# Padded full-array pair units, a transposed second batch and DMA transposes in a recurrence + mixer kernel

## The chip, the cores and the metric

The kernel runs on one core of one Trainium2 chip. The metric is the device time of one execution in microseconds (us). Before the change the median of three runs is 174.36 us (174.34 to 175.11). A profiled run took 174.75 us; the profile's span, from its first to its last instruction, is 173.0 us, and all positions below are counted from the start of that span.

## The reference

Two parts follow each other. The first is a gated linear recurrence for 4 batches, 8 heads, 768 time steps and a head width of 48. The second is a low-rank mixing over time and an MLP over the 384 channels.

```python
# q, k, v, alpha: (4, 8, 768, 48)
for t in range(S):
    state = alpha[:, :, t, :, None] * state + outer(k[:, :, t], v[:, :, t])   # per batch and head
    y[:, :, t] = q[:, :, t] @ state
x = y as (B, S, 384)
h = (x^T @ U @ V)^T            # U: (768, 32), V: (32, 768)
u = x + h
out = u + max(u @ w_ch1, 0) @ w_ch2      # w_ch1: (384, 1536), w_ch2: (1536, 384)
```

The kernel computes the recurrence in chunks: with the running product of alpha folded into q and k, a chunk's output is q times the state before the chunk, plus a masked (q k^T) times v, and the state is carried on once per chunk.

## The kernel before

Work is not issued in program order. Each operation is added to a plan with the engines that may do it and an estimated cost; the plan then simulates the engines and fixes the order of each engine's instructions before anything is built. A buffer is taken from a pool when the plan reaches its first user. TensorE's modes (whole array, halves, quarters) cost a switch in the plan.

```python
LAT = {"PE": 215.0, "ACT": 155.0, "DVE": 145.0, "POOL": 110.0, "SP": 400.0}
SWITCH = 95.0
TOL = 150.0
...
P.warm_until = 28000.0      # until then gaps on TensorE are filled with products of zeros (line 291)
```

Batches 0 and 1 (`PAIR`) are cut in units of 256 time steps and four heads, two time steps to a partition (j = 0, 1). The two halves of the partitions are two chunks (c = 0, 1) of 128 steps. State update and output are products over 64 partitions, each half into a bank of its own:

```python
P.add({"POOL": 480, "ACT": 420}, lambda e: copy(e, jh(rv()), raw(vt)), ...)         # v to bf16, rows kt, rv
...
db = [Buf(bank) for _ in range(nch)]            # nch = 2 for the first two blocks, 1 for the last
for n in range(4):
    a, j = n // 2, n % 2
    for c in range(nch):
        r = slice(64 * c, 64 * c + 64)
        nc.tensor.matmul(db[c]()[:, a * 2 * D : (a + 1) * 2 * D],                   # line 479
            lhsT=rk()[r, HP * j + 2 * a : HP * j + 2 * a + 2, :]..., rhs=rv()[r, ...]...)
...
yb = Buf(bank), Buf(bank)
# q times the state before the chunk: line 518, 96 columns, whole array
for h in range(HP):
    for j in range(2):
        for c in range(2):
            r = slice(64 * c, 64 * c + 64)
            nc.tensor.matmul(yb[c]()[:, h * D : (h + 1) * D],                       # line 531
                lhsT=pm()[r, (h // 2) * 2 + j, h % 2, :], rhs=rv()[r, HP * j + h, :], ...)
for c in range(2):    # two copies of 192 columns to xb
    P.add({"ACT": 250, "DVE": 265}, ...)
```

Batches 2 and 3 are cut in units of 128 steps and eight heads. In both kinds of unit alpha's logarithm is taken on ScalarE (lines 375 and 547), summed over time on TensorE (384 to 391, 554 to 557), and its exponentials scale k and q to `rk` and `rq` (405, 572). These are transposed on TensorE (418, 584) and copied from PSUM to `kt` and `qt`. Then come the scores (445, 605), their mask on VectorE (456, 615), the state and the output (for batches 2 and 3 lines 628, 662 and 664).

The mixing reads the finished batch (line 681: x times U). Batch 0 builds u transposed directly in PSUM, from products with the identity (700) and the low-rank term (703), and a second time untransposed for the residual. The other batches build u untransposed and transpose it on TensorE:

```python
for c in range(NC):
    hb = Buf(bank, 3 if b == 0 else 0)
    P.add({"PE": mm(DM)}, ... vm_sb x utx ...)                  # line 712
    P.add({"DVE": 465}, ... ub = xb + hb ...)                   # line 713
    if c % 2 == 1 and b > 0:
        ...
        P.add({"PE": mm(*[C] * 6)}, f_tr, ...)                  # line 722: six transposes of 128x128
        P.add({"DVE": 450, "ACT": 710}, f_ev, ...)              # copy to uT
```

The MLP's first stage (line 749) takes 72 products of 384 columns for a batch, with a ReLU out of PSUM on ScalarE or VectorE (759, 761). The second stage (line 772) takes another 72, and VectorE adds the residual (779):

```python
nc.tensor.matmul(hb()[:, 0:TW], lhsT=w1_sb[:, ct, ...], rhs=uT()[:, ct, ...], ...)          # line 749
...
nc.tensor.matmul(hb()[:, 0:DM], lhsT=h1()[:, jt, ...], rhs=w2_sb[:, jt, :], ...)            # line 772
...
P.add({"DVE": 468}, lambda e: nc.vector.tensor_tensor(ou(), ub()[:, c, :], hb()[:, 0:DM], op=ALU.add), ...)
P.add({"SP": 550.0}, lambda e: nc.sync.dma_start(out[b, c * C : (c + 1) * C, :], ou()), ...)
```

All DMAs are issued by SyncE (SP), in the plan's order.

Of the kernel before, what the change touches and what calls it, by code (L numbers as in the profile page):

```python
# [40 lines left out]
class Plan:  # L41
# [4 lines left out]
    TOL = 150.0  # L46
    warm = None
# [41 lines left out]
    def run(self):  # L89
# [10 lines left out]
        while todo:  # L100
# [18 lines left out]
            for eng, ok in per.items():  # L119
                t0 = min(t for t, _ in ok)  # L120
                t1, op = min(((t, o) for t, o in ok if t <= t0 + 1.0), key=lambda x: (x[1].prio, x[1].i))
                key = (t1, t1 + op.engs[eng])
                if best is None or key < best[0]:
                    best = (key, eng, op)
# [12 lines left out]
            if eng == "SP":  # L137
                dma = max(dma, t + 600.0) + cost
                clock[eng] = max(t + 450.0, dma - 3500.0)
                end = dma + 2000.0  # L140
            else:
                if eng == "PE" and op.mode != mode:
                    cost += self.SWITCH
                    mode = op.mode
                clock[eng] = end = t + cost
            order.append(op)
            done = end + self.LAT[eng]
            for b in op.bufs:
                b.left -= 1
                b.last = max(b.last, done)  # L150
                if b.left == 0:
                    b.pool.free[b.idx] = b.last
# [27 lines left out]
def kernel(  # L180
# [33 lines left out]
    PAIR = (0, 1)  # L214
    RES = (1, 1, 1, 0)
# [55 lines left out]
    rvs = Pool(slots("rv", 5, [C, H, D], BF16))  # L271
# [9 lines left out]
    ubs = Pool(slots("ub", 3, [128, NC, DM], BF16))  # L281
# [22 lines left out]
    def small():  # L304
        P.add({"SP": 450.0}, lambda e: nc.sync.dma_start(u_in, moe_U.rearrange("(c p) r -> p c r", p=128)), w=["u_in"], prio=2.5)
        P.add({"SP": 500.0}, lambda e: nc.sync.dma_start(v_in, moe_V), w=["v_in"], prio=2.5)
# [8 lines left out]
    def weight(dst, src, key, prio, pr, engs):  # L315
        t = Buf(io)
        P.add({"SP": 540.0}, lambda e: nc.sync.dma_start(flat(t), src), w=[t], prio=prio)  # L317
        P.add(engs, lambda e: copy(e, dst, flat(t)), r=[t], w=[key], prio=pr)
# [14 lines left out]
    LEAD = 3.0  # L333
    tiles = {}

    def stage_loads(b):
        def load(t, src, c, key):
            if b in PAIR:
                hs, sl = slice((c % 2) * HP, (c % 2 + 1) * HP), slice((c // 2) * 2 * C, (c // 2 + 1) * 2 * C)
                P.add(  # L340
                    {"SP": 750.0},
# [7 lines left out]
            P.add({"SP": 1000.0}, lambda e: nc.sync.dma_start(t(), src[b, :, sl, :].rearrange("h t d -> t h d")), w=[t], prio=key)  # L349
# [11 lines left out]
    def stage_pair(b, u, sprev, xb):  # L361
# [3 lines left out]
        sl = 0.0 if b == 0 else 150.0  # L365
# [10 lines left out]
        rv = Buf(rvs)  # L376
        P.add({"POOL": 480, "ACT": 420}, lambda e: copy(e, jh(rv()), raw(vt)), r=[vt], w=[rv], prio=pr + 20, slack=sl)
# [85 lines left out]
        db = [Buf(bank) for _ in range(nch)]  # L463
# [6 lines left out]
        def f_id(e, c, last):  # L470
            nc.tensor.matmul(db[c]()[:, 0 : 2 * Q // 2], lhsT=ident, rhs=sview(before[c]), start=not last, stop=last, skip_group_check=True)

        def f_d(e):
            for n in range(4):
                a, j = n // 2, n % 2
                for c in range(nch):
                    r = slice(64 * c, 64 * c + 64)
                    more = onpe and c == 1
                    nc.tensor.matmul(
                        db[c]()[:, a * 2 * D : (a + 1) * 2 * D],  # L480
                        lhsT=rk()[r, HP * j + 2 * a : HP * j + 2 * a + 2, :].rearrange("t h w -> t (h w)"),
                        rhs=rv()[r, HP * j + 2 * a : HP * j + 2 * a + 2, :].rearrange("t h d -> t (h d)"),
                        start=(n == 0 and not (onpe and c == 0 and sprev is not None)), stop=(n == 3 and not more), skip_group_check=True,
                    )

        if onpe and sprev is not None:
            P.add({"PE": mm(Q)}, lambda e: f_id(e, 0, False), r=[(sprev, 1)], w=[db[0]], prio=pr + 8, slack=sl)
        P.add({"PE": mm(*[2 * D] * 4)}, f_d, r=[rk, rv], w=db, prio=pr + 8, mode="H", slack=sl)
        for c in range(nch):
# [10 lines left out]
            if onpe or prev is None:  # L500
                if onpe and c == 1:
                    P.add({"PE": mm(Q)}, lambda e: f_id(e, 1, True), r=[(st, 0)], w=[db[1]], prio=pr + 7, slack=sl)
                P.add({"DVE": 270}, lambda e, c=c, f=f_st: f(e, db[c]()[:, 0:Q]), r=[db[c], tot], w=[(st, c)], prio=pr + 4, slack=sl)
            else:
                sm = Buf(sms)
                P.add(
                    {"DVE": 270},
                    lambda e, c=c, sm=sm, prev=prev: nc.vector.tensor_tensor(sm()[:, 0:Q], db[c]()[:, 0:Q], sview(prev), op=ALU.add),
                    r=[db[c], prev], w=[sm], prio=pr + 4, slack=sl,
                )  # L510
                P.add({"POOL": 480, "DVE": 270}, lambda e, sm=sm, f=f_st: f(e, sm()[:, 0:Q]), r=[sm, tot], w=[(st, c)], prio=pr + 4, slack=sl)

        yb = Buf(bank), Buf(bank)

        def f_yi(e, c):
            s = before[c]
            for a in range(2):
                nc.tensor.matmul(
                    yb[c]()[:, 2 * a * D : (2 * a + 2) * D], lhsT=qT()[:, 2 * a + c, :], rhs=s[0]()[:, 2 * s[1] + a, :],
                    start=(a == 0), stop=False, skip_group_check=True,  # L520
                )

        def f_y(e):
            for c in range(2):
                if before[c] is not None:
                    f_yi(e, c)
            for h in range(HP):
                for j in range(2):
                    for c in range(2):
                        r = slice(64 * c, 64 * c + 64)  # L530
                        nc.tensor.matmul(
                            yb[c]()[:, h * D : (h + 1) * D], lhsT=pm()[r, (h // 2) * 2 + j, h % 2, :], rhs=rv()[r, HP * j + h, :],
                            start=(h == 0 and j == 0 and before[c] is None), stop=(h == HP - 1 and j == 1), skip_group_check=True,
                        )

        P.add({"PE": mm(*[2 * D] * 4, *[D] * 8) + 95}, f_y, r=[qT, rv, (pm, 0), (pm, 1)] + [x for x in before if x is not None], w=[yb[0], yb[1]], prio=pr, mode="H", slack=sl)
        for c in range(2):
            P.add({"ACT": 250, "DVE": 265}, lambda e, c=c: copy(e, xb()[:, 2 * blk + c, half * Q : (half + 1) * Q], yb[c]()[:, 0:Q]), r=[yb[c]], w=[(xb, 2 * blk + c, half)], prio=pr, slack=sl)
        return st

    def stage_gla(b, c, sprev, xb):
        kk = b * NC + c
        pr = kk * 100.0
        sl = 150.0
# [33 lines left out]
        tk, tq = Buf(bank), Buf(bank)  # L578
        kT, qT = Buf(kts), Buf(qts)

        def f_tr(ring, tb):
            t = bf(tb()).rearrange("p (e c) -> p e c", c=C)
            for p in range(HP):
                nc.tensor.matmul(  # L584
                    t[:, p, :],
                    lhsT=ring()[:, 2 * p : 2 * p + 2, :].rearrange("t h w -> t (h w)"),
                    rhs=ident, start=True, stop=True, is_transpose=True,
                )

        def f_ev(e, dst, tb):  # L590
            copy(e, dst(), bf(tb()).rearrange("p (e c) -> p e c", c=C)[:, 0:HP, :])

        P.add({"PE": mm(*[C] * 4)}, lambda e: f_tr(rk, tk), r=[rk], w=[tk], prio=pr + 18, slack=sl)
        P.add({"PE": mm(*[C] * 4)}, lambda e: f_tr(rq, tq), r=[rq], w=[tq], prio=pr + 18, slack=sl)
        P.add({"DVE": 335, "ACT": 500}, lambda e: f_ev(e, kT, tk), r=[tk], w=[kT], prio=pr + 8, slack=sl)
        P.add({"DVE": 335, "ACT": 500}, lambda e: f_ev(e, qT, tq), r=[tq], w=[qT], prio=pr + 8, slack=sl)
# [76 lines left out]
    def stage_mix(b, xb, ub, uT):  # L673
        pr = (b * NC + NC - 0.5) * 100.0
        sl = 0.0 if b == 0 else 150.0
# [10 lines left out]
        if b == 0:  # L686
# [6 lines left out]
        if b == 0:  # L693
# [15 lines left out]
            pr = mlp_prio(0, 0.3)  # L709
        for c in range(NC):  # L710
            hb = Buf(bank, 3 if b == 0 else 0)
            P.add({"PE": mm(DM)}, lambda e, c=c, hb=hb: nc.tensor.matmul(hb()[:, 0:DM], lhsT=vm_sb[:, c * C : (c + 1) * C], rhs=utx(), start=True, stop=True), r=[utx, ("vm", c // NT)], w=[hb], prio=pr + c, slack=sl)  # L712
            P.add({"DVE": 465}, lambda e, c=c, hb=hb: nc.vector.tensor_tensor(ub()[:, c, :], xb()[:, c, :], hb()[:, 0:DM], op=ALU.add), r=[hb] + xk(b, xb, c), w=[(ub, c)], prio=pr + c, slack=sl)  # L713
            if c % 2 == 1 and b > 0:
# [18 lines left out]

    def mlp_prio(b, x):
        return ((b + 1) * NC + LEAD + x * NC) * 100.0

    def mlp1(b, uT, h1, tt):
        for jt in range(NJ):
# [3 lines left out]
            if b == 0:  # L742
                need = [(uT, tt, j) for j in range(NCT)]
            else:
# [20 lines left out]
    def mlp2(b, ub, h1, c):  # L765
        hb = Buf(bank, RES[b])
        tt = c // NT
        for g in range(3):

            def f(e, g=g):  # L770
                for jt in range(4 * g, 4 * g + 4):
                    nc.tensor.matmul(  # L772
                        hb()[:, 0:DM], lhsT=h1()[:, jt, c * C : (c + 1) * C], rhs=w2_sb[:, jt, :],
                        start=(jt == 0), stop=(jt == NJ - 1),
                    )

            P.add({"PE": mm(*[DM] * 4)}, f, r=[(h1, tt, jt) for jt in range(4 * g, 4 * g + 4)] + [("w2", jt) for jt in range(4 * g, 4 * g + 4)], w=[hb], prio=mlp_prio(b, 0.5 + c / 12.0 + g / 36.0))
        ou = Buf(outs)
        P.add({"DVE": 468}, lambda e: nc.vector.tensor_tensor(ou(), ub()[:, c, :], hb()[:, 0:DM], op=ALU.add), r=[hb, (ub, c)], w=[ou], prio=-100)  # L779
# [7 lines left out]
    for b in range(B):  # L787
# [7 lines left out]
        stage_mix(b, xb, ub, uT)  # L795
        mlp1(b, uT, h1, 0)
        mlp1(b, uT, h1, 1)
        for c in range(NC):
            mlp2(b, ub, h1, c)
# [33 lines left out]
```

## Time and profile before

| What | Value |
|---|---|
| Median time | 174.36 us |
| Span of the profile | 173.0 us, mean granted TensorE clock 0.986 |
| MLP products (lines 749 and 772) | 288 + 288, 53.1 + 52.8 us in the rows |
| Transposing products (418, 584, 700, 722) | 96 + 96 + 18 + 54 |
| Half-array products (479, 531) | 80 + 192 |
| Additions for u on VectorE (713) | 24, 547 ns each |
| Copies of v on GpSimd | 19, 590 ns each |
| Loads of q, k, v, alpha and the weights | 120 of 192 KB, 4.3 to 4.5 us from issue to landing |
| Output stores | 24 of 192 KB, 1.9 us |

Busy times are given for each engine over the span. PE is TensorE's products, PEld its weight loads, which lie beside the products. DVE is VectorE, ACT ScalarE, POOL GpSimd and SPq the sequencer of SyncE, which only issues DMAs. The profile cuts the span in 40 slices of 4.3 us and gives the busy share of each in tenths. Products on TensorE overlap like a pipeline, so the duration of one in a row is its latency and not the time that it takes from the engine. The chain of waits follows the work that ended last back from its end, at each step to what released it. Windows give busy times by stage.

### The profile page before, as it was taken

Reading aid. Unit: us, or ns where it says so; the run is one execution under the profiler, and the core shown is the slowest. Engines: PE = TensorE matmul, PEld = TensorE weight load, DVE = VectorE, ACT = ScalarE, POOL = GpSimd, SP = SyncE. Lnnn points to the kernel's source line nnn. Section 1 sums busy time; section 2 is a strip of 40 time slices with the busy share of each in tenths; the row PEclk is TensorE's granted clock in tenths of the full one; section 3 lists DMA queues with packets and bytes.
Section 4 is the critical chain, followed back from the end, with each engine's and each line's share of the span. In section 5 each row is a group of like instructions: output and inputs, shape, how many; then the busy total and the mean of one; then the engine's idle time right before and its main releaser. Section 6 shows DMA issues by size and latency. Waiting matters only on the chain.

```text
span 173.0 us, 4823 instructions
## 1 busy us (share of the span) xinstructions
PE 161.9 (94%) x1862; PEld 104.2 (60%) x1862; DVE 109.0 (63%) x232; ACT 104.1 (60%) x247; POOL 59.5 (34%) x97
## 2 busy tenths in 40 slices
PE   7688998899996999999998999999999999999991
PEld 2355765566564776676676657666666566656560
DVE  4589685598996986958675559976474294000231
ACT  4588773779785767558949436638783210996000
POOL 8056366247331765255155414910430000000000
PEclk9999699999999999999999999999999999999998
DMA  5999989999998999999989999611000212100222
GB/s 140 266 249 260 267 255 335 258 300 330 269 267 200 178 207 211 214 222 221 230 147 206 189 166 258 170 58 37 0 0 4 91 45 91 51 0 0 91 93 91
DMA packets 83031, 28.82 MB, mean 167 GB/s; under 512 B 76832, under 2 KB 82976, under 8 KB 83008
## 3 DMA queue, kind: packets, MB, share of 16 engines
q1 hardware_dynamic: 83008, 28.52, 72.0%
q8 instruction: 14, 0.23, 0.6%
q14 instruction: 9, 0.07, 0.2%
HBM read 23.79 MB, written 4.72 MB: 165 GB/s over the span
## 4 chain that ended last, share of the span: by engine, by line
PE 60%; DMA 19%; SPq 15%; issue 2%; POOL 1%; ACT 1%; DVE 0%; ACTq 0%; POOLq 0%
PE ps L772 27%; PE ps L749 16%; SPq L342 10%; DMA io<-in_v_dram 8%; DMA io<-in_moe_w_ch_dram 5%; SPq L317 3%; DMA io<-in_alpha_dram 3%; PE ps L584 3%; DMA io<-in_k_dram 3%; PE ps L605 2%; PE ps L712 2%; PE ps L722 2%; PE ps L664 1%; PE ps L554 1%; PE ps L418 1%
## 5 line engine op out<-in xcount | busy, mean ns | idle before, releaser
L749 PE MATMUL ps<-uT,w_sb 128*128 128x384 bf16 x288 | 53.1, 326 | 0.0
L772 PE MATMUL ps<-w_sb,h1t 128*128 128x384 bf16 x288 | 52.8, 326 | 0.0
L759 ACT ACTIVATE h1t<-ps 128x384 bf16<-128x384 f32 x73 | 35.2, 494 | 8.8 <-PE ps L749 8.5
L772 PEld LDWEIGHTS <-h1t 128*128 128x128 bf16 x288 | 26.1, 98 | 16.0 <-issue 1.0
L749 PEld LDWEIGHTS <-w_sb 128*128 128x128 bf16 x288 | 26.1, 98 | 15.4
L779 DVE TENSOR_TENSOR ou<-ub,ps 128x384 f32<-128x384 bf16 x24 | 13.2, 551 | 27.6 <-PE ps L772 27.3
L302 POOL CAST rv<-io 128x384 bf16<-128x384 f32 x19 | 11.2, 590 | 35.7 <-DMA io<-in_v_dram 30.7
L615 DVE TENSOR_TENSOR pm<-ps,maskc 128x512 bf16<-128x512 f32 x24 | 15.7, 685 | 6.7 <-PE ps L605 6.5
L572 POOL TENSOR_TENSOR rk<-io,ai 128x384 bf16<-128x384 f32 x12 | 11.0, 916 | 20.2 <-ACT ai L565 18.7
L761 DVE TENSOR_SCALAR h1t<-ps 128x384 bf16<-128x384 f32 x23 | 12.6, 552 | 7.4 <-PE ps L749 4.8
L456 DVE TENSOR_TENSOR pm<-ps,maskp 128x512 bf16<-128x512 f32 x24 | 15.8, 681 | 0.7 <-ACT h1t L759 0.5
L298 ACT CAST xb<-ps 128x192 bf16<-128x192 f32 (+1 forms) x23 | 8.8, 392 | 11.6 <-PE ps L664 7.6
L298 ACT COPY kt<-ps 128x512 bf16<-128x512 bf16 x17 | 10.0, 586 | 5.8 <-PE ps L584 5.3
L713 DVE TENSOR_TENSOR ub<-xb,ps 128x384 bf16<-128x384 bf16 x24 | 12.1, 547 | 1.2 <-PE ps L712 1.2
L298 ACT COPY qt<-ps 128x512 bf16<-128x512 bf16 x17 | 11.3, 663 | 1.6 <-PE ps L418 1.0
L302 POOL CAST w_sb<-io 128x384 bf16<-128x384 f32 x21 | 10.8, 527 | 3.8 <-DMA io<-in_moe_w_ch_dram 3.5
L572 POOL TENSOR_TENSOR rq<-io,aa 128x384 bf16<-128x384 f32 x12 | 11.6, 967 | 0.0
L375 ACT ACTIVATE lt<-io 128x384 bf16<-128x384 f32 x12 | 6.4, 530 | 5.2 <-DMA io<-in_alpha_dram 5.2
L298 ACT COPY uT<-ps 128x768 bf16<-128x768 bf16 x4 | 3.2, 799 | 8.6 <-PE ps L722 5.1
L547 ACT ACTIVATE lt<-io 128x384 bf16<-128x384 f32 x12 | 6.5, 542 | 2.0 <-DMA io<-in_alpha_dram 2.0
L398 ACT ACTIVATE ai<-ps 128x384 bf16<-128x384 f32 x12 | 5.9, 493 | 2.8 <-PE ps L391 2.8
L565 ACT ACTIVATE ai<-ps 128x384 bf16<-128x384 f32 x12 | 6.0, 500 | 2.4 <-PE ps L557 2.0
(114 smaller groups left out, 249.3 us busy)
## 6 DMA issues: line engine op xcount, KB each, us to landing
io<-in_alpha_dram SPq DMA_DIRECT2D x24, 192.0 KB, 4.3
io<-in_k_dram SPq DMA_DIRECT2D x24, 192.0 KB, 4.5
io<-in_q_dram SPq DMA_DIRECT2D x24, 192.0 KB, 4.3
io<-in_v_dram SPq DMA_DIRECT2D x24, 192.0 KB, 4.5
io<-in_moe_w_ch_dram SPq DMA_DIRECT2D x24, 192.0 KB, 4.4
out_dram<-ou SPq DMA_DIRECT2D x24, 192.0 KB, 1.9
u_in<-in_moe_U_dram SPq DMA_DIRECT2D x1, 96.0 KB, 4.6
v_in<-in_moe_V_dram SPq DMA_DIRECT2D x1, 96.0 KB, 4.3
```

Of the source, the lines that this page charges most:

```text
L298: nc.scalar.copy(dst, src)
L302: nc.gpsimd.tensor_copy(dst, src)
L342: lambda e: nc.sync.dma_start(t().rearrange("p (h j) d -> p h (j d)", j=2), src[b, hs, sl, :].rearrange("h (p j) d -> p h (j d)", j=2)),
L456: nc.vector.tensor_tensor(dst, s2, maskp.to_broadcast([C, 2, 2, C]), op=ALU.mult)
L572: eng.tensor_tensor(dst()[:, :, 0:D], a(), x(), op=ALU.mult)
L615: nc.vector.tensor_tensor(pm()[:, :, par, :], s2, maskc.to_broadcast([C, HP, C]), op=ALU.mult)
L713: P.add({"DVE": 465}, lambda e, c=c, hb=hb: nc.vector.tensor_tensor(ub()[:, c, :], xb()[:, c, :], hb()[:, 0:DM], op=ALU.add), r=[hb] + xk( ...
L749: nc.tensor.matmul(hb()[:, 0:TW], lhsT=w1_sb[:, ct, jt * 128 : (jt + 1) * 128], rhs=uT()[:, ct, tt * TW : (tt + 1) * TW], start=(ct == 0), ...
L759: nc.scalar.activation(dst, hb()[:, 0:TW], AF.Relu)
L761: nc.vector.tensor_scalar_max(dst, hb()[:, 0:TW], 0.0)
L772: nc.tensor.matmul(hb()[:, 0:DM], lhsT=h1()[:, jt, c * C : (c + 1) * C], rhs=w2_sb[:, jt, :], start=(jt == 0), stop=(jt == NJ - 1),)
L779: P.add({"DVE": 468}, lambda e: nc.vector.tensor_tensor(ou(), ub()[:, c, :], hb()[:, 0:DM], op=ALU.add), r=[hb, (ub, c)], w=[ou], prio=-100)
```

## The change

It has five parts, and the constants of the plan are set anew with them.

1. In the pair units v is copied to a tile with zeros in the other half (`rw`), so that one product over all 128 partitions gives both chunks side by side in one bank. The half-array mode is gone from these two places, and a unit holds seven banks where it held nine.
2. Batch 1 too builds u transposed in PSUM (`XT = (0, 1)`). For batches 0 and 1 the untransposed u is no longer made: the output stage takes the low-rank term as a 13th product, and adds x.
3. The transposes of k and q of the last four units of batch 3 are DMAs issued by SyncE (`TRD`).
4. So are those of u in batch 3 (`TRU`).
5. The plan: costs of loads are raised, a buffer is taken to be free 200 ns later (`EASE`), work after batch 0 gets 300 instead of 150 ns of slack, a change of TensorE's mode lowers an operation's rank by 20, the MLP comes one unit later in rank (`LEAD`), and U and V are loaded later.

The core of the diff (cuts are marked with ...):

```diff
-                t1, op = min(((t, o) for t, o in ok if t <= t0 + 1.0), key=lambda x: (x[1].prio, x[1].i))
+                t1, op = min(((t, o) for t, o in ok if t <= t0 + 1.0), key=lambda x: (x[1].prio + (self.STAY if eng == "PE" and x[1].mode != mode else 0.0), x[1].i))
...
+            if eng == "SP" and op.mode == "X":
+                dma = max(dma, t) + cost
+                clock[eng] = t + cost
+                end = dma + 850.0
...
-                b.last = max(b.last, done)
+                b.last = max(b.last, done + self.EASE)
...
+    TRD = {(3, c) for c in range(2, NC)}
+    SL = 300.0
+    TRU = (3,)
+    XT = (0, 1)
...
-    rvs = Pool(slots("rv", 5, [C, H, D], BF16))
+    rvs = Pool(slots("rv", 4, [C, H, D], BF16))
+    rv2_s = slots("rw", 4, [C, 2, HP, 2, D], BF16)
+    for x in rv2_s:
+        nc.gpsimd.memset(x, 0.0)
...
-    LEAD = 3.0
+    LEAD = 4.0
...
+        def f_rv(e, c):
+            r = slice(64 * c, 64 * c + 64)
+            copy(e, rv()[r, :, :, c, :], raw(vt)[r])
+        for c in range(2):
+            P.add({"POOL": 480, "ACT": 420}, lambda e, c=c: f_rv(e, c), r=[vt], w=[(rv, c)], prio=pr + 20, slack=sl)
...
-        db = [Buf(bank) for _ in range(nch)]
+        db = Buf(bank)
...
+                nc.tensor.matmul(
+                    out[:, 0:nch, a, :].rearrange("p c (h d) -> p c h d", h=2),
+                    lhsT=rk()[:, HP * j + 2 * a : HP * j + 2 * a + 2, :].rearrange("t h w -> t (h w)"),
+                    rhs=rv()[:, j, 2 * a : 2 * a + 2, 0:nch, :].rearrange("t h c d -> t c h d"),
+                    start=(n == 0), stop=(n == 3 and not onpe), skip_group_check=True,
+                )
...
+                    nc.tensor.matmul(
+                        y[:, :, h, :], lhsT=pm()[:, (h // 2) * 2 + j, h % 2, :], rhs=rv()[:, j, h, :, :],
+                        start=False, stop=(h == HP - 1 and j == 1), skip_group_check=True,
+                    )
...
+        if (b, c) in TRD:
+            for ring, dst in ((rk, kT), (rq, qT)):
+                P.add({"SP": 1250.0}, lambda e, ring=ring, dst=dst: nc.sync.dma_start(dst(), ring().rearrange("t h w -> t (h w)"), transpose=True), ...)
...
-        if b == 0:
+        if b in XT:
...
+            if b in TRU:
+                P.add({"SP": 1250.0}, lambda e, c=c: nc.sync.dma_start(uT()[:, :, c * C : (c + 1) * C], ub()[:, c, :], transpose=True), ...)
...
+                if low:      # batches 0 and 1, last third of the output stage
+                    nc.tensor.matmul(hb()[:, 0:DM], lhsT=vm_sb[:, c * C : (c + 1) * C], rhs=utx(), start=False, stop=True)
...
-        P.add({"DVE": 468}, lambda e: nc.vector.tensor_tensor(ou(), ub()[:, c, :], hb()[:, 0:DM], op=ALU.add), ...)
+        P.add({"DVE": 468}, lambda e: nc.vector.tensor_tensor(ou(), (xb if b in XT else ub)()[:, c, :], hb()[:, 0:DM], op=ALU.add), ...)
```

## The prediction

> **What bounds the kernel now.** I read the busy times first, then the 40 slices, then the chain of waits, then the windows by stage.
>
> ```profile
> PE 161.9 (94%) x1862; PEld 104.2 (60%) x1862; DVE 109.0 (63%) x232; ACT 104.1 (60%) x247; POOL 59.5 (34%) x97
> ...
> PE   7688998899996999999998999999999999999991
> ...
> DMA  5999989999998999999989999611000212100222
> ...
> PE 60%; DMA 19%; SPq 15%; issue 2%; POOL 1%; ACT 1%; DVE 0%; ACTq 0%; POOLq 0%
> ```
>
> TensorE is far ahead of the other engines. The DMA slices show that the inputs arrive until about slice 25 (108 us). The windows cut the span where I see stages end:
>
> ```profile
> core 0: us, PE busy (x) PEld busy (x) DVE busy (x) ACT busy (x) POOL busy (x), PEclk, DMA share, GB/s
> 0.00:30.70 30.70, 25.99 (x404) 16.49 (x405) 21.32 (x60) 20.05 (x49) 16.41 (x39) 0.94 1.03 254
> 30.70:91.00 60.30, 57.90 (x757) 38.14 (x756) 48.38 (x100) 43.44 (x107) 27.64 (x40) 1.00 1.04 232
> 91.00:146.00 55.00, 54.54 (x560) 35.64 (x560) 35.48 (x66) 28.92 (x69) 15.41 (x19) 1.00 0.50 101
> ```
>
> Until 30.7 us batch 0 passes through its recurrence as fast as its loads land, and TensorE is filled up with warming products. At 30.69 the first MLP product (L749) starts, and from there TensorE is next to full until 169.5. The chain of waits in order of time ends like this:
>
> ```profile
> 130.85 0.22 PE ps L584 x4
> 131.07 1.30 PE ps L772 x8
> 132.37 0.33 PE ps L605 x8
> ...
> 135.58 0.20 PE ps L664 x8
> ...
> 146.10 11.70 PE ps L749 x72
> 157.80 11.71 PE ps L772 x72
> ```
>
> It holds no wait at all: product follows product. A row's mean (326 ns for 384 columns) is a latency; the slot that a product takes is a piece of this chain divided by its count. So **slot prices**: 384 columns 1.30/8 = 0.1625 us; 128 columns 0.22/4 = 0.056; 48 columns 0.20/8 = 0.025; the groups of four with 96 columns (L628, 0.17) 0.0425 each; 192 columns about 0.083 (L385 starts 0.09 before L386).
>
> [...]
>
> ```profile
> 36.36 0.65 PE L749 MATMUL ps<-uT,w_sb 128*128 128x384 bf16 x3
> 36.94 0.34 PE L479 MATMUL ps<-rv,rk 64*128 64x96 bf16 x8
> 37.22 0.66 PE L749 MATMUL ps<-uT,w_sb 128*128 128x384 bf16 x3
> ```
>
> Three 384s end their slots at 36.36 + 0.49 = 36.85, but the half-array group starts at 36.94; its eight products, two at a time, need 4 x 0.0425 = 0.17 and take 0.28. So there are about 0.09 + 0.11 us of switching around one such group. [...] An ordinary output store of 192 KB lands in a median 1.9 us here.
>
> **The change, part by part**, in TensorE slots over the whole kernel, with counts from the built order of instructions of both kernels.
>
> 1. Half-array products become full-array ones (12 pair units). State update before: 0.17 + 0.2 switching = 0.37 each, 12 x 0.37 = 4.4 us. After: 32 products of 192 columns and 16 of 96: 32 x 0.083 + 16 x 0.0425 = 3.3. Output before: 192 half products two at a time, 12 x (0.20 + 0.2) = 4.8; after, 96 products of 96 columns, 4.1. (The 40 state terms of 96 columns stay.) So the padding doubles the columns per unit of useful work, and what is gained is the switching: **-1.8 us**, at most, half of it in batch 0, where TensorE isn't the bound.
>
> 2. Batch 1 gets its u by transposing products into PSUM with the low-rank term added there. L700 goes from 18 to 36 and L722 loses 18, the same width: 0. L703 goes from 6 to 12: +6 x 0.1625 = **+1.0**. The six L712 of batches 0 and 1 each become a 13th product of the output stage: 0. VectorE loses 12 additions (L713, 547 ns): -6.6 us.
>
> 3. Batch 3's u is transposed by DMA: -18 x 0.056 = **-1.0**. So are k and q of its last four units: -32 x 0.056 = **-1.8**. Eight copies from PSUM (rows kt, qt: about 0.42 to 0.66 us) and three uT copies go from ScalarE and VectorE: some 6 us off both together.
>
> 4. v is copied in two half-partition pieces, each still 384 elements long: 24 copies instead of 12, about +12 x 0.55 = 6.6 us on GpSimd and ScalarE. Four memsets of the padded tiles: a 128x512 memset takes 0.53 (L239), so about 0.8 each, 3.2 us. GpSimd is idle from 4.3 to 8.6 us (its first rv waits 4.29 us for DMA), so these are hidden.
>
> 5. The two 192-column output copies become one: 24 of about 0.33 to 12 of about 0.48: -2 us on ScalarE and VectorE. One bank instead of two for states and outputs: a pair unit holds seven banks, not nine.
>
> 6. The planner's constants (slower loads, 200 ns more before a buffer is taken to be free, 300 instead of 150 ns slack, a penalty for switching mode) move work about. The order of loads barely changes.
>
> Sum of TensorE slots: -1.8 + 1.0 - 1.0 - 1.8 = **-3.6 us**. The whole before: MLP 576 x 0.1625 = 93.6; 56 more 384s 9.1; 32 192s 2.6; 264 transposes 14.7; 120 tiny ones 3.0; 24 score groups of 0.33 to 0.35, 8.2; L681 1.75; pair units 4.4 + 4.8 + 1.7; the other units' states and outputs 5.8; together 149.7. Of these, 16.6 stand ahead of the first L749 (decay sums 2.7, transposes 2.7, scores 2.1, states 2.9, outputs 3.2, batch 0's mixing 3.0). After, 15.6 do, so 1.0 of the gain lies in the load-bound start and is worth nothing. Before: 149.7 - 16.6 = 133.1 us of slots in 138.8 us (30.69 to 169.5), so **5.7 us of holes**. After: 133.1 - 2.6 = 130.5.
>
> The list of waits names what can be closed of the holes: 1.46 us at 54.0 (L479 waits for rv, which waits for a v load), 0.74 at 32.6 (a Ln that waits for alpha) and 0.63 at 91.5 (qt, behind a Ln that waits for alpha). That is 2.8 us. The rest are switches and short joints. With 13 us less on VectorE and ScalarE together, fewer banks and a plan with truer load times I expect about 1.5 us of the 2.8 to go. The start and the end (169.5 to 173.0: last addition, store) stay.
>
> So: 174.4 - 2.6 - 1.5 = **170.3 us**.
>
> **Rivals.** (a) *TensorE stays the bound and the holes stay*: 174.4 - 2.6 = 171.8. For it: the holes are made by loads, and the bytes are the same. (b) *The DMA transposes put a wait in TensorE's way.* SyncE issues in order, so a transpose that waits for rk also holds back the last loads and the stores behind it. In the built order, after the last transposed unit's decay sums, there stand 33 L749-products (5.4 us), two score groups (0.66) and two output groups (0.74) ahead of its scores: 6.8 us. The unit's own path is two Exp (0.9), rk and rq on GpSimd (0.92 + 0.97) and a transpose, about 2 us if it is like a store: 4.8. That leaves 2 us. If a transpose takes 5 us instead, four units could lose 1 to 2 us each: 174 to 178. Against it: the last u transposes have 36 output products (5.9 us) ahead of the first product that needs them. (c) *The start gets later*: ScalarE takes 15 of the 24 v pieces, most in the first 28 us, where it is already 20 of 30.7 us busy. If the first MLP product slips by 1 us, so does the end. (d) *The plan closes nearly all holes*: 168 to 169. For it: the list of waits for TensorE holds few entries, all with a load behind them.
>
> **Range and chances.** (a) and the middle lie at 170 to 172, (d) at 168 to 169, (b) and (c) at 172 and up. I choose 170.3 and 167.0 to 173.3 for 8 in 10. The border for faster is 174.36 x 0.98 = 170.9, close to my middle; (d) seems to me likelier than (b), as the constants look as if they had been set from measured loads. Faster 0.57, same 0.36, slower 0.07.
>
> **What would show it.** First L749-product at 30 to 31 us, whatever its new line: step 4 right. No half-array groups (64*128) in the TensorE rows of the pair units and no gaps of 0.1 around them: step 1. 1699 instead of 1862 products, of which 9 more are warming ones. VectorE near 100 us, ScalarE under 104. Transposes to land in 2 to 3 us, and no wait of TensorE for qt, kt or uT from a DMA over 0.5 us in the last 60 us: otherwise (b). The sum of TensorE's named waits after 31 us at about 1.3 us: if it is still 2.8, (a). The last 144 products should still take 23.4 us. The prediction is wrong if a transpose lands in over 4 us, or if a new wait on the v copies appears early in batch 0 or 1.

## The result and the profile after

The changed kernel takes 172.59 us (median; 172.52 to 173.27) where the kernel before takes 174.6 us in the same comparison (174.34 to 175.11): a ratio of 0.9891, interval 0.9854 to 0.9927. The direction and the range of the prediction held. But the gain of 1.1% is a little less than half of the 2.3% that I had forecast, and the gain of over 2%, to which I had given 0.57, did not come.

The busy times of the changed kernel, its row of 40 slices for TensorE, and the shares of its chain of waits:

```profile
PE 159.0 (93%) x1694; PEld 103.7 (61%) x1699; DVE 107.5 (63%) x214; ACT 104.0 (61%) x242; POOL 61.6 (36%) x104
...
PE   7288788899999999999999999999999999999992
...
PE 81%; DVE 2%; ACT 1%; issue 1%
```

In the PE row the middle is now all nines, where before it had a 6 and an 8; but the second slice is a 2 where it was a 6. The chain consists of TensorE products for 81% of the span; before, DMA and SyncE had a third of it. The windows by stage, with the same cuts as before (us, then busy time and instructions of each engine):

```profile
core 0: us, PE busy (x) PEld busy (x) DVE busy (x) ACT busy (x) POOL busy (x), PEclk, DMA share, GB/s
0.00:30.70 30.70, 22.80 (x304) 14.83 (x309) 23.09 (x54) 19.72 (x45) 17.41 (x39) 0.94 1.07 259
30.70:91.00 60.30, 59.77 (x736) 41.47 (x736) 48.04 (x94) 46.16 (x113) 29.00 (x46) 1.00 1.00 224
91.00:146.00 55.00, 55.00 (x526) 34.69 (x524) 33.08 (x62) 27.85 (x65) 15.17 (x21) 1.00 0.70 136
```

TensorE's gaps after 30.7 us have shrunk from 2.4 + 0.5 to 0.5 + 0, while in the first stage it is busy 3.2 us less. So the change gained more in its middle than I had forecast and lost something at the start. The timeline of the changed kernel's start shows what (start, duration, engine, line and operation; in brackets the idle time ahead and what ended it):

```profile
3.01 4.04 DVE L254 COPY maskp<-mask 64x256 bf16<-64x256 bf16 x1 [0.93 <-POOL mask L250]
...
4.21 2.76 POOL L284 MEMSET rw<- 128x768 bf16 x4
7.06 0.22 DVE L255 COPY maskp<-mask 64x256 bf16<-64x256 bf16 x1
...
8.00 0.17 PE L407 MATMUL ps<-offd,ident 128*128 128x8 bf16 x1 [3.14 <-DVE offd L269]
```

Two copies of the same shape stand on VectorE. The second takes 0.22 us, the first 4.04: it ends at 7.05, 0.08 us after the last of the four new memsets on GpSimd (4.21 + 2.76 = 6.97). `offd`, a small constant that VectorE makes behind the copies, is late too, and TensorE's product at L407, a part of the first decay sums, waits 3.14 us for it. In the timeline of the kernel before the copy took 1.10 us and the same product (there L387) started at 5.08:

```profile
3.02 1.10 DVE L244 COPY maskp<-mask 64x256 bf16<-64x256 bf16 x1 [0.93 <-POOL mask L240]
...
3.55 0.48 POOL L268 MEMSET rq<- 128x128 bf16 x3
...
5.08 0.17 PE L387 MATMUL ps<-offd,ident 128*128 128x8 bf16 x1 [0.28 <-DVE offd L259]
```

To keep accounts I cut every profile in the same way. The **first** MLP product starts; the **end** is that of the last MLP product (start of the last 72 in the chain plus 11.71 us); the stretch between them is filled with slots at the prices of the prediction; what is left are holes.

| Kernel | First | End | Stretch | Slots | Holes |
|---|---|---|---|---|---|
| Before | 30.69 | 169.51 | 138.8 | 133.1 | 5.7 |
| After | 34.36 | 167.46 | 133.1 | 130.5 | 2.6 |

Forecast were -2.6 us of slots, -1.5 of holes and nothing at the start: -4.1. The profile shows -2.6, -3.1 and **+3.7**: -2.0, which is also the difference of the medians (174.6 - 172.59).

### The profile page after: what moved, and what is told of

It is laid out like the page before. It is cut to its first block, busy times and chain, and to the rows that moved or that the text cites. A ratio compares the mean times of both kernels' runs of the same rounds, so it can differ in the third digit from the quotient of the medians.

```text
span 170.8 us, 4498 instructions
## 1 busy us (share of the span) xinstructions
PE 159.0 (93%) x1694; PEld 103.7 (61%) x1699; DVE 107.5 (63%) x214; ACT 104.0 (61%) x242; POOL 61.6 (36%) x104
## 4 chain that ended last, share of the span: by engine, by line
PE 81%; DVE 2%; ACT 1%; issue 1%
PE ps L785 28%; PE ps L810 28%; PE ps L631 2%; PE ps L610 2%; PE ps L438 2%; PE ps L546 2%; PE ps L465 1%; PE ps L690 1%; PE ps L572 1%; PE ps L729 1%; PE ps L738 1%; PE ps L815 1%; PE ps L688 1%; PE ps L497 1%; PE ps L707 1%; PE ps L654 1%
## 5 line engine op out<-in xcount | busy, mean ns | idle before, releaser
L819 DVE TENSOR_TENSOR ou<-ub,ps 128x384 f32<-128x384 bf16 x12 | 6.6, 554 | 27.6 <-PE ps L810 27.6
L797 DVE TENSOR_SCALAR h1t<-ps 128x384 bf16<-128x384 f32 x26 | 14.1, 555 | 5.6 <-PE ps L785 5.5
L312 ACT CAST xb<-ps 128x384 bf16<-128x384 f32 x19 | 9.1, 480 | 8.3 <-PE ps L690 5.0
L590 POOL TENSOR_TENSOR rq<-io,aa 128x384 bf16<-128x384 f32 x12 | 11.3, 940 | 0.0
L418 ACT ACTIVATE ai<-ps 128x384 bf16<-128x384 f32 x12 | 5.9, 493 | 8.6 <-PE ps L411 8.3
L819 DVE TENSOR_TENSOR ou<-xb,ps 128x384 f32<-128x384 bf16 x12 | 6.6, 553 | 7.1 <-PE ps L815 6.4
L425 POOL TENSOR_TENSOR rq<-io,aa 128x384 bf16<-128x384 f32 x6 | 5.7, 950 | 11.2 <-ACT aa L419 5.6
L316 POOL CAST w_sb<-io 128x384 bf16<-128x384 f32 x20 | 9.3, 509 | 0.7 <-DMA io<-in_moe_w_ch_dram 0.6
L305 PE MATMUL ps<-filler 128*128 128x512 bf16 x18 | 7.5, 518 | 1.5 <-DVE filler L237 1.2
L314 DVE COPY qt<-ps 128x512 bf16<-128x512 bf16 x10 | 6.4, 638 | 2.7 <-PE ps L438 1.7
L312 ACT CAST rw<-io 64x384 bf16<-64x384 f32 x15 | 7.6, 507 | 0.2
L312 ACT COPY qt<-ps 128x512 bf16<-128x512 bf16 x10 | 6.6, 660 | 1.2 <-PE ps L438 1.0
```

What stands on the lines that cost most here:

```text
L305: P.warm = lambda: nc.tensor.matmul(ps[:, 7, :], lhsT=filler[:, 0:128], rhs=filler, start=True, stop=True)
L312: nc.scalar.copy(dst, src)
L314: nc.vector.tensor_copy(dst, src)
L316: nc.gpsimd.tensor_copy(dst, src)
L590: eng.tensor_tensor(dst()[:, :, 0:D], a(), x(), op=ALU.mult)
L797: nc.vector.tensor_scalar_max(dst, hb()[:, 0:TW], 0.0)
```

## The experiments

Theory A: the memsets that I had put down as hidden hold VectorE's copy and so the start, and this is the missing gain. Rival B: the start isn't what counts, because loads set the pace afterwards and TensorE would only wait later. Theory P: the extra holes were closed by the plan's constants, not by parts 1 to 4. For each run the ratio to the kernel before on the same chip is given; on the three chips of the experiments the median of that kernel is 175.39 us (e1 to e4), 175.72 (e5 to e8) and 175.02 (e9 to e12).

**The start.** *e1*: the changed kernel, with the two mask copies on ScalarE instead of VectorE; the memsets stay.

```diff
-    nc.vector.tensor_copy(maskp[0:64, 0], mask2[0:64, :, 0:C])
-    nc.vector.tensor_copy(maskp[64:128, 0], mask2[64:128, :, C : 2 * C])
+    nc.scalar.copy(maskp[0:64, 0], mask2[0:64, :, 0:C])
+    nc.scalar.copy(maskp[64:128, 0], mask2[64:128, :, C : 2 * C])
```

> The changed kernel with one thing different: the two small copies that build maskp run on ScalarE instead of VectorE; the order on every other engine is the same. Theory A (the late start is the loss): VectorE's copy waited behind GpSimd's four new memsets, so without it the first decay constants are ready near 5 us instead of 8, the first MLP product moves from 34.4 to about 31.5 us and the end follows by the same 3 us: 169.5 us against 172.6. Rival B (the start was covered anyway, and the holes come back): the first MLP product starts earlier, but TensorE then runs into loads that land no earlier, its holes grow from 2.6 towards 5.7 us, and the time stays at 172 to 172.6. Rival C (the copies of v on ScalarE[...] make the start late): the first MLP product stays after 33.5 us and the time at 172.5.

Measured: 169.08 us (169.01 to 169.58), ratio 0.9622 (0.9558 to 0.9686). The timeline of e1's start:

```profile
3.01 0.41 ACT L254 COPY maskp<-mask 64x256 bf16<-64x256 bf16 x1 [0.99 <-POOL mask L250]
...
4.18 2.76 POOL L284 MEMSET rw<- 128x768 bf16 x4
...
5.01 0.21 PE L407 MATMUL ps<-offd,ident 128*128 128x8 bf16 x1
...
5.37 0.49 ACT L418 ACTIVATE ai<-ps 128x384 bf16<-128x384 f32 x1 [1.00 <-PE ps L411]
...
5.89 0.56 DVE L425 TENSOR_TENSOR rk<-io,ai 128x384 bf16<-128x384 f32 x1 [2.60 <-ACT ai L418]
```

On ScalarE the same copy takes 0.41 us and is over before the four memsets begin, and L407 starts at 5.01 instead of 8.00. Not all work is held up by the memsets: an exponential on ScalarE (L418) and even a multiplication on VectorE (L425) start and end while they run, in 0.49 and 0.56 us. The first MLP product starts at 30.85 (-3.5) and the last ends at 164.46 (-3.0). Theory A holds for the changed kernel, and this is **the fastest version found, ahead of both kernels**.

*e2*: the kernel before, with the same four memsets (of 128x768 elements, on tiles that are written later anyway). *e3*: the kernel before, with e1's edit.

```diff
+    for x in (ut_s[0][:, 0, :], ut_s[0][:, 1, :], ut_s[1][:, 0, :], ut_s[1][:, 1, :]):
+        nc.gpsimd.memset(x, 0.0)
```

> The kernel before with only the suspected cost added: four memsets of 128x768 bf16 on GpSimd at the place of the setup where the changed kernel has them, on tiles that are not yet in use. Theory A: VectorE's copy to maskp takes about 4 us instead of 1.1, the first MLP product moves from 30.7 to about 33.5 us, and the time rises by 2.5 to 3 us, to 177.3. Rival B: the first MLP product moves, but TensorE's holes close and the time rises by less than 1 us. Rival C: GpSimd is idle there, so nothing moves: 174.6 us.

> The kernel before with the two maskp copies on ScalarE. In it the copy took 1.10 us on VectorE where its twin took 0.23, and the first decay sums waited 0.28 us for VectorE's constants. Theory A: the start gains 0.3 to 0.9 us and the time with it: 173.8 to 174.2. Rival B: loads set the pace, no change, 174.5.

Measured: e2 175.83 us, 1.0031 (1.0002 to 1.0059); e3 175.94 us, 1.0035 (1.0005 to 1.0065). The timeline of e2 has the same blocked copy:

```profile
3.01 4.04 DVE L244 COPY maskp<-mask 64x256 bf16<-64x256 bf16 x1 [0.93 <-POOL mask L240]
```

Four memsets alone thus delay the setup. But in e2's profile the first MLP product is 2.5 us late (33.16) and the end is not (169.03): its holes fall from 5.7 to 2.8. By the ratio, 0.3%, about 0.5 us of the 2.5 remains. In e3 the reverse happens, which neither expectation had: the start is 0.7 us earlier, and the list of TensorE's waits after 30 us holds four of 1.0 to 1.3 us (qt, a logarithm, utx, h1t, all behind ScalarE), 4.6 in sum, where the kernel before has 2.8.

So rival B is right for the kernel before. In these two kernels a late start costs only where nothing later would have waited anyway, and the changed kernel is of that kind.

**The plan's constants.** *e5*: the kernel before with the new constants alone. *e6*: e1 with all the old ones.

```diff
 # e5 (shortened), on the kernel before; e6 is the reverse, on e1
+    EASE = 200.0; STAY = 20.0     # buffer free later; rank lowered by a change of mode
-    SL = 150.0
+    SL = 300.0
-    LEAD = 3.0
+    LEAD = 4.0
-    # planned cost of loads (SP): 540, 750, 1000
+    # 590, 790, 1080; U and V later in rank (2.5 -> 4.5)
```

> The kernel before with only the plan's constants of the changed kernel (dearer loads, buffers free 200 ns later, 300 ns slack, mode penalty 20, LEAD 4, U and V later): same operations, other order. From the first MLP product to the last, the kernel before took 138.8 us for 133.1 us of slots, the changed one 133.1 us for 130.5. Theory P (the plan's constants close the holes): the stretch falls to about 136 us and the time to 171.7 to 172.5. Rival Q (the holes close because VectorE, ScalarE and banks are freed by the other parts): the stretch stays at 138 to 139 us, the time at 174.5 to 175.5.

> The changed kernel with maskp on ScalarE (169.1 us), but with the plan's constants of the kernel before. Theory P: the holes grow from 3.1 to 5.5 us, the time to 171.5. Rival Q: the holes stay, 169 to 169.5.

Measured: e5 172.17 us, 0.9792 (0.9732 to 0.9851); e6 176.41 us, 0.9991 (0.9959 to 1.0024), a greater loss than I expected. Of the three waits listed for the kernel before (1.5 for rv, 0.7 and 0.6), e5 keeps one:

```profile
PE ps L386 <- ACT lt L377: 0.5, 1, 0.5
```

Theory P holds: constants that change only the order of the work, and which engine takes a piece of it, are worth 2.1% by themselves. With 0.9792, e5 is even ahead of the changed kernel and its 0.9891. And without them parts 1 to 4, even with e1's undisturbed start, are worth nothing that these runs can tell. With them, parts 1 to 4 and e1's edit add 1.7% (0.9622 against 0.9792). The parts need the constants; the constants pay without the parts, too.

*e9, e10, e11*: e1 with one group of the old constants each.

```diff
-    LEAD = 4.0                      # e9
+    LEAD = 3.0
-    # load costs 590, 790, 1080     # e10
+    # 540, 750, 1000
-    EASE = 200.0; SL = 300.0        # e11
+    EASE = 0.0; SL = 150.0
```

> The changed kernel with maskp on ScalarE (169.1 us; with all old constants of the plan 176.4), only LEAD back to 3. If LEAD is the constant that matters (the MLP of a batch comes one unit later in rank, so products that depend on no load remain as filling), most of the 7 us comes back: 173 to 176 us. Otherwise 169 to 170.5.

> The same kernel, only the plan's costs of loads back to the old ones (540, 750, 1000 instead of 590, 790, 1080). In the plan 120 loads then end some 7 to 9 us earlier than they do now, so that TensorE's order counts on data that is not there: if this is what matters, waits for rw, lt and qt appear and the time is 172 to 175 us. Otherwise 169 to 170.

> The same kernel, only the slack constants back: buffers free at once instead of 200 ns later, 150 instead of 300 ns of slack after batch 0. If tolerance of small delays is what matters: many short waits and 171 to 174 us. Otherwise 169 to 170.

Measured: e9 172.79 us, 0.9895 (0.982 to 0.997); e10 173.27 us, 0.9911 (0.9884 to 0.9939); e11 169.32 us, 0.9695 (0.9652 to 0.9738), whose trace is level with e1's. The slack isn't what matters; LEAD and the load costs are: 3.7 and 4.2 us by the medians, 2.7% and 2.9% by the ratios. They work in different ways. In e10 DMAs and their issue stand in the chain of waits again, with 31% of the span (34% before), and TensorE's largest waits after 31 us (engine, line, releaser: us in total, times, longest) lie in the middle, between 90 and 106 us:

```profile
PE ps L654 <- POOL rk L590: 1.2, 1, 1.2
PE ps L810 <- ACT xb L312: 1.1, 1, 1.1
```

In e9 there is one wait, at the end. Its chain of waits (start, us, what) and its windows there:

```profile
140.93 2.31 DMA uT<-ub
143.38 13.54 PE ps L785 x72
```

```profile
140.00:143.38 3.38, 0.57 (x4) 0.14 (x3) 1.09 (x3) 0.00 (x0) 0.00 (x0) 1.00 0.50 128
...
144.00:148.00 4.00, 4.00 (x17) 1.97 (x15) 0.00 (x0) 2.33 (x5) 0.00 (x0) 0.57 0.39 76
148.00:157.00 9.00, 9.00 (x57) 5.44 (x56) 0.00 (x0) 8.94 (x20) 0.00 (x0) 1.00 0.01 2
```

The changed kernel has kept 36 output products back, 5.85 us, that cover the transposing DMA of the last u:

```profile
138.20 5.85 PE ps L810 x36
144.05 11.70 PE ps L785 x72
```

With LEAD 3 they have been used up earlier, only eight at the end are left, and TensorE stands still for 2.81 us. The granted clock, the third figure from the end, is 1.00 in the window of the wait, 0.57 in the 4 us from 144 on, and 1.00 again after that. The 72 products behind the wait take 13.54 us where they take 11.70 in the changed kernel: another 1.84 us. This was not so each time: two of e9's four executions have a mean granted clock of 1.00 and took 171.9 us, 2.8 more than e1's median; the other two, the profiled one among them, have 0.99 and took 173.7 and 173.9. What decides between the two isn't shown.

**The parts on TensorE and SyncE.** *e4*: the changed kernel with the transposes of parts 3 and 4 back on TensorE. *e12*: e1 with the u of batch 2 by DMA as well.

```diff
-    TRD = {(3, c) for c in range(2, NC)}     # e4
-    TRU = (3,)
+    TRD = set()
+    TRU = ()
-    TRU = (3,)                               # e12
+    TRU = (2, 3)
```

> The changed kernel without DMA transposes: k, q and u of batch 3 are transposed on TensorE again and copied from PSUM. If TensorE's slots set the time from the first MLP product on, 50 more products of 128 columns cost 50 x 0.056 = 2.8 us: 175.4 us. Rival: they were hidden in holes, or the DMA transposes cost as much elsewhere: under 1 us, 172.6 to 173.4. The first MLP product should start at 34.4 us as in the changed kernel.

> The same kernel, with u of batch 2 also transposed by DMA. By the slots: 18 products of 128 columns fewer, -1.0 us, 168.1. Rival: near 100 to 108 us the loads of batch 3 still fill the DMA queues, a transpose takes 4 us or more to land instead of 2.3 and holds the loads behind it back: a wait for uT and 170 us or more.

Measured: e4 175.76 us, 1.0034 (1.0006 to 1.0062); its slots rise by 2.8 us (18 + 32 products of 0.056) and so does its stretch, from 133.1 to 135.9, with the holes unchanged at 2.6. Where TensorE is full, a slot is worth its price. e12 took 176.66 us, 1.0107 (1.0074 to 1.0141): 1.0 us of slots fewer, and 7.7 us of holes more than e1. SyncE's own timeline in e12:

```profile
101.49 3.90 SPq L743 DMA_TRANSPOSE uT<-ub  x3
...
123.91 0.99 SPq L363 DMA_DIRECT2D io<-in_v_dram  x1
```

A transpose of u keeps SyncE's issue for 1.18 to 1.75 us (median 1.21), most loads between 85 and 130 us for 0.4 to 1.1 (two for 2.2). Six more of them come between and the last unit's loads of q and v follow only at 123.21 and 123.91; in the changed kernel they leave at 112.53 and 113.01:

```profile
113.01 0.68 SPq L363 DMA_DIRECT2D io<-in_v_dram  x1
```

The u transposes themselves land after a median of 2.4 us (3.8 at most), not the 4 or more of my rival; it is the order of issue that holds the loads back. Everything behind is late, and at the end TensorE waits again for the last u:

```profile
PE ps L785 <- DMA uT<-ub: 4.9, 1, 4.9
```

The 72 products after it take 14.00 us instead of 11.70; the mean granted clock of this execution is 0.978, and where in it the clock was lower isn't shown. This is rival (b) of the prediction, which the changed kernel avoids by using SyncE for one batch only.

*e7*: e1 with the pair units of the kernel before (half-array products, nine banks, v in one copy, no memsets). *e8*: e1 with only batch 0 built transposed.

```diff
-    def stage_pair(...):            # e7 (shortened): rw, products of 192 columns, seven banks
+    def stage_pair(...):            # that of the kernel before; rw and its memsets gone, 5 rv
-    XT = (0, 1)                     # e8
+    XT = (0,)
```

> The changed kernel with maskp on ScalarE, but its pair units as in the kernel before: half-array products, nine banks, v in one copy, no padded tiles and no memsets. By the slots, batch 1 loses 0.9 us of switching saved and batch 0's share is covered: 170.0 us. Rival: the two banks matter more, because nine of eight cannot be held at once: holes too, 171 or more. Other rival: v in one copy frees ScalarE in the start and makes up for it: 169.0 or less.

> The changed kernel with maskp on ScalarE, but batch 1 builds u as in the kernel before: 6 products of 384 columns fewer on TensorE (-1.0 us of slots), 6 more additions on VectorE (+3.3 us) and a longer chain from the last unit to the MLP. If the slots decide: 168.1 us. Rival: VectorE and the chain open holes of more than that, 169.5 to 170.5 us, which would be what this part is for.

Measured: e7 171.65 us (170.42 to 172.89), 0.9758 (0.9677 to 0.9839); e8 170.0 us, 0.9675 (0.96 to 0.975). In e7's profile the stretch is 1.1 us longer than e1's, of which 0.9 is the slots and switches that the prediction priced for batch 1; its one listed wait of TensorE is 0.9 us for a transposing DMA of q. Its median is 2.6 us above e1's and its runs are spread over 2.5 us, so the size of part 1 stays open between 0.9 and 2.6 us. In e8 the slots fall by 1.0 us as priced, but the holes grow by 1.1 (one is a wait of 0.6 us for VectorE's masked scores, pm), as VectorE and ScalarE together are busy 2.1 us longer (103.9 + 106.8 against 103.7 + 104.9); the median is 0.9 us above e1's, though the intervals of the two ratios overlap. That part 2's extra products pay for themselves through the work that they take off these two engines is what this points to, not more.

All profiles in the same account:

| Kernel | First | End | Slots | Holes |
|---|---|---|---|---|
| e1, mask on ScalarE | 30.85 | 164.46 | 130.5 | 3.1 |
| e2, before + memsets | 33.16 | 169.03 | 133.1 | 2.8 |
| e3, before, mask on ScalarE | 29.97 | 171.02 | 133.1 | 7.9 |
| e4, transposes on TensorE | 34.36 | 170.24 | 133.3 | 2.6 |
| e5, before, new plan | 30.54 | 167.31 | 133.1 | 3.7 |
| e7, e1, half-array pairs | 30.61 | 165.30 | 131.4 | 3.3 |
| e8, e1, batch 1 untransposed | 30.85 | 164.60 | 129.5 | 4.2 |
| e9, e1, LEAD 3 | 30.89 | 168.63 | 130.5 | 7.2 |
| e10, e1, old load costs | 30.29 | 168.36 | 130.5 | 7.6 |
| e11, e1, old slack | 30.61 | 163.70 | 130.5 | 2.6 |
| e12, e1, u of batch 2 by DMA | 30.85 | 171.19 | 129.5 | 10.8 |

Each row is one execution: those of e2 and e7 took 1.5 and 1.2 us less than their medians, so that their holes come out small by about as much, and that of e6, 1.9 us above its median, is left out. The holes of e9 and e12 contain the 1.84 and 2.30 us by which the 72 products behind the wait for the last u take longer than 11.70.

## Why the prediction was right and where it was wrong

**Right: the slots (steps 1, 2, 3 and their sum).** The stretch has 2.6 us of slots fewer, and e4 gave 2.8 us back for its 50 transposes, to the tenth. The number of products is 1699 by their weight loads (1694 in the row of PE, where a few can be missing), and the last 144 take 11.70 + 11.71 = 23.4 us. The switching is gone: in the changed kernel's TensorE timeline the group that stood with 0.09 and 0.11 us around it before

```profile
41.07 0.65 PE L785 MATMUL ps<-uT,w_sb 128*128 128x384 bf16 x3
41.56 0.49 PE L497 MATMUL ps<-rw,rk 128*128 128x192 bf16 x4
41.89 0.65 PE L785 MATMUL ps<-uT,w_sb 128*128 128x384 bf16 x3
```

starts at 41.07 + 3 x 0.1625 = 41.56 and gives way after 4 x 0.083 = 0.33, at 41.89.

**Right: rival (b) stays away.** The transposes land in 2.3 to 2.9 us (DMA issues; the last column is the median from issue to landing). The 2 us of the prediction were an estimate from the 1.9 us of a store; a store takes 2.1 here. In the changed kernel no wait of TensorE is listed after 34.3 us at all.

```profile
uT<-ub SPq DMA_TRANSPOSE x6, 2.3
kt<-rk SPq DMA_TRANSPOSE x4, 2.9
qt<-rq SPq DMA_TRANSPOSE x4, 2.4
```

**Wrong: step 4, GpSimd "idle from 4.3 to 8.6 us" and the memsets "hidden".** I asked who needs GpSimd in that time, and not who else is held up while GpSimd works. The memsets themselves take 2.76 us (3.2 were estimated), but they aren't hidden. My sign for this step, the first MLP product at 30 to 31 us, came at 34.36, 3.7 us late. The memsets alone make 2.5 us of that in the kernel before (e2), and e1 gave 3.5 back in the changed one. Rival (c) had a later start but blamed ScalarE's copies of v; ScalarE is busy 19.72 us in the first stage, no more than before (20.05). A part of (c) stays open, though: with like against like, the changed kernel still starts later than the kernel before, by 1.2 us with the memsets in both (34.36 against e2's 33.16) and by 0.9 with the mask on ScalarE in both (30.85 against e3's 29.97). No run shows what does that. What becomes of VectorE's copy is in the trace: 4.04 us against 0.22 for the same copy without a GpSimd neighbour, ended 0.08 us after the memsets, and it did not get in between two of them. By what mechanism GpSimd holds it, no run shows. The trace of before had the sign already: the same copy took 1.10 us beside four small copies and three memsets on GpSimd (2.93 to 4.03 us), and I read over it. This also accounts for VectorE at 107.5 instead of about 100 us: 3.8 of it is the blocked copy, and e1 has 103.7. The other 3.7 us is my estimate of the work removed, which was too high; so was that for ScalarE, at 104.0 just short of "under 104".

**Wrong in size: the holes, by step 6, constants that "move work about".** I took about half of the 2.8 us of named waits; all of them went, and 3.1 us of holes. Part of this can be the late start itself, which leaves the loads more time (e2's profile has 2.9 us of holes less by nothing else). But e1 starts early and still has only 3.1 us of holes, and in e5 the constants alone take 2.0 us. Rival (d) described the middle of the kernel correctly: 174.4 - 2.6 - 2.6 is 169.2, and e1, in which the memsets don't hold the start up, takes 169.08. Its reason, constants set "from measured loads", isn't shown: e10 shows that the dearer loads pay, not that they are truer. The two errors had opposite signs; by that luck the total lay inside the range.

**Not tested.** The penalty for a change of mode and the later loading of U and V were changed together with the other constants only, in e5 and e6.

## What to carry to other kernels

Before new work on an "idle" engine is called hidden, look at what its neighbours do in that time: a duration of 4.04 us in a row where the same shape takes 0.22 is a wait in disguise. Moving the victim to ScalarE gave 2.7% where the start set the end, and 0.3% the other way in the kernel before, where it did not. A microsecond at the start is worth a microsecond only if no later wait takes it back, so ask first where the kernel would take it back (e2 against e1). In a kernel that is ordered by a cost model, the assumed load costs and a reserve of independent products for the end can be worth more than the instructions saved, and have to be tried as a part of the change by themselves.

## What the runs showed of the hardware

- GpSimd work with four memsets at its end, one behind the other, holds a VectorE bf16 copy of 64x256 from its start at 3.01 us to the end of the last memset (4.04 us instead of 0.22), with memsets on two different sets of tiles (after and e2). Beside the four memsets, ScalarE's exponentials of 128x384 take 0.49 us and VectorE's multiplications of 128x384 0.56 us (e1).
- A transposing DMA of a 128-partition tile between on-chip tiles costs about 1.2 us of SyncE's issue (medians 1.19 to 1.21 in the changed kernel, 1.21 for u in e12) and lands after 2.3 to 2.9 us in the median (2.4 in e12).
- A wait of TensorE of 2.81 us near the end goes, in e9's profiled execution, with a granted clock of 0.57 in a window of 4 us that begins 0.6 us after its end, and the following 72 products take 1.84 us longer; two of e9's four executions keep a mean clock of 1.00. After a wait of 4.9 us (e12) they take 2.3 us longer (14.00 - 11.70), with a mean clock of 0.978 over the execution.
